# Pooled attention and a spatial gating unit on one core: gated units over other batches, and PSUM divided anew

## The chip, the cores and the metric

The kernel is one program on 1 core of one Trainium2 chip. A core has five engines with instruction queues of their own: TensorE (PE, matmuls, with weight loads shown apart as PEld), VectorE (DVE), ScalarE (ACT), GpSimd (POOL) and SyncE (SP, which here issues all DMA transfers). Each executes its own queue in order; semaphores tie the queues together. TensorE writes its products to PSUM, which the kernel divides into eight banks of 128 partitions x 512 float32; VectorE and ScalarE read them there. The metric is device microseconds for the whole program, as the median of several runs. One further execution is profiled; its instructions, with start and end, are the trace.

## The reference

What is computed is an attention with pooled queries, followed by a gated feed-forward block with a product over the sequence:

```python
q_pool = q.reshape(B, H, S // 2, 2, D).mean(axis=3)          # B=8, H=8, S=1152, D=64
scores = 1/sqrt(D) * q_pool @ k^T                            # 576 x 1152 for each batch and head
attn = exp(scores - max) / (sum + 1e-9)
x = (attn @ v), heads side by side                           # 8 x 576 x 512
h = maximum(x @ w_in, 0);  u, v = halves of h                # 512 columns each
v_n = (v - mean) / sqrt(var + 1e-6)                          # over the 512 columns
v_s = einsum('ts,bsd->btd', w_spatial, v_n) + b_spatial[None, :, None]   # over the 576 rows
out = (u * v_s) @ w_out                                      # 8 x 576 x 512
```

Inputs and outputs are float32, `w_in` and `w_out` come as 64-bit numbers whose two halves the kernel unpacks itself. To keep precision, a matrix that enters TensorE is split into a float16 head and a float16 rest, and most products are sums of three matmuls (head x head, head x rest, rest x head).

## The kernel before, in words

**Pairs.** The attention is done in 32 *pairs* of heads (8 batches, 4 pairs each). `attention(i)` (L487 on) makes the scores of pair i in 18 steps: for each, two matmuls of 512 columns (L506, L507) into a bank `pss`, an exponential on ScalarE (L512) and, for two steps together, a subtraction on GpSimd that makes the rest (L524). The remaining 64 query columns of each head go through four short `tail_tile`s (L520). `values` (L428, L432, L435) multiplies the exponentials with v into the bank `o`, four steps later; VectorE divides (`xm`, L443). `turn_main` (L457, L463) transposes a finished pair into `xg`, the input of the gated part (ScalarE L401, VectorE L402). `tail_values` (L478 to L480) does the short columns, in 27 matmuls.

**Beside each pair** small generators are advanced at fixed rates, once or more per *tick* (a pair has 40): `maxima` of the next pair (27 matmuls of 384 columns, L342 and L333, each reduced by VectorE at L348), `prep` of the pair after that (splitting q and k, with a scale that comes from a sum over partitions by TensorE, `scales`, L112), `values_ahead` (v), and until pair 8 `load_weights`, which fetches 512 x 512-column pieces of `w_in` and `w_out`, unpacks each with six VectorE and two ScalarE instructions (`from_double`, L149 to L161; the piece's staging is double-buffered) and splits it into head and rest (L135, L138). It is advanced by 0.25 steps a tick.

**Gated units.** A unit takes two batches, [0,1], [2,3], [4,5], [6,7]. `gated_unit` is a generator too: v products in nine row tiles (L582; ScalarE L590 evacuates, VectorE takes statistics at L592, L593), u products in 12 column pieces (L646, evacuated by ScalarE at L656) with the normalisation of v between (VectorE L618, L624, ScalarE L623), eight spatial products (L688 for 512 and L689 for 64 columns, into two banks at once; VectorE L695, L698), `split` (a scale of the gated product, `scale_of`, then head L135 and rest L138), output products in nine tiles (L731, evacuated by ScalarE at L751) and stores. A unit becomes ready when its last pair is transposed, and half a step of the oldest ready unit is made per tick; the unit's 160 or so steps so fill the eight pairs that follow. The last unit has no pairs beside it: it runs after pair 31, in two groups whose second scale lies behind the first group's products, and takes its banks from `pss` too.

**PSUM.** Eight banks: three `pss` (scores), two `pm` (maxima, scales, transposes, short columns), one `o`, two `pw` (units; while no unit is ready, every second maximum too).

**Order.** The code is written as one sequence, but a scheduler then sets the order on each engine: it keeps program order as priority and brings ready work forward, by its own estimate of durations and by which banks and buffers are free.

## Time and profile before

| | us |
|---|---|
| median of 3 runs | 1376.04 |
| lowest, highest | 1375.12, 1377.23 |
| the profiled execution | 1378.83 |
| its span, first to last instruction | 1377.1 |

| engine | busy us | share of the span | instructions |
|---|---|---|---|
| PE (matmuls) | 1222.1 | 89% | 13696 |
| PEld (weight loads) | 741.5 | 54% | 13696 |
| DVE | 967.1 | 70% | 2068 |
| ACT | 970.6 | 70% | 1632 |
| POOL | 847.0 | 62% | 492 |

Of the busy times it has to be known that matmuls are pipelined: a matmul's duration reaches from its start to its modelled end, and the next one starts long before that. So the distance from start to start, not the duration, is what a matmul takes of TensorE, and a busy TensorE is not one at its peak. The page's share is a mean over stages, so the stages are told apart with windows. In a row of a group, after the shapes and the count, stand the busy time and the mean of one in ns, then the time for which the engine had nothing to do before these instructions and what ended it. Waits are put down to what came last.

### The profile page before, as it was taken

The numbers are of one execution on the slowest core, as the hardware profiler recorded it, in microseconds if no ns is written. First come the engines' busy times: TensorE is split into PE (matmuls) and PEld (weight loads), VectorE is DVE, ScalarE is ACT, GpSimd is POOL, SyncE is SP. The second block draws the span as 40 slices with busy tenths as digits, with TensorE's granted clock in tenths as the row PEclk, the third lists the DMA queues.
The fourth block names the chain that finished last, engine by engine and source line by source line (L and its number), as shares of the span: only waits on it lengthen the run. The fifth ranks groups of instructions, "written<-read, shape, count | busy, mean of one in ns | idle before, by whom it ended". The sixth has DMA issues, their size and how long they took to land.

```text
span 1377.1 us, 33478 instructions
## 1 busy us (share of the span) xinstructions
PE 1222.1 (89%) x13696; PEld 741.5 (54%) x13696; DVE 967.1 (70%) x2068; ACT 970.6 (70%) x1632; POOL 847.0 (62%) x492
## 2 busy tenths in 40 slices
PE   3677887788998999889998999889998999899998
PEld 1354555555554665556555666555555566556443
DVE  5799889986869767765668766775667866761455
ACT  6777678779966777768776886768776776655333
POOL 3587677878755666657774766667666576655000
PEclk9998899989999999999999999999999999999999
DMA  7533343434333231244332132244331131101002
GB/s 252 166 97 109 94 124 94 128 93 139 113 96 96 79 94 56 62 126 135 96 96 87 51 91 84 74 118 135 104 96 42 47 94 55 28 24 40 8 1 69
DMA packets 56346, 123.77 MB, mean 90 GB/s; under 512 B 8256, under 2 KB 16448, under 8 KB 56192
## 3 DMA queue, kind: packets, MB, share of 16 engines
q1 hardware_dynamic: 56192, 121.63, 29.8%
q8 instruction: 107, 1.75, 0.5%
q14 instruction: 47, 0.39, 0.1%
HBM read 83.56 MB, written 9.44 MB: 68 GB/s over the span
## 4 chain that ended last, share of the span: by engine, by line
PE 47%; DVE 25%; ACT 8%; POOL 7%; DMA 7%; issue 4%; SPq 1%; POOLq 0%; ACTq 0%; DVEq 0%
DVE mt L348 7%; PE pss L507 5%; PE pss L506 5%; PE pw L688 5%; POOL pt L524 4%; PE pm L342 4%; PE pw L731 4%; PE pw L646 3%; PE o L435 3%; PE o L428 3%; PE pw L582 3%; ACT pt L512 3%; DMA kq<-in_qT_dram 3%; PE o L432 3%; DVE vv L138 2%
## 5 line engine op out<-in xcount | busy, mean ns | idle before, releaser
L524 POOL TENSOR_TENSOR pt<-pt 128x1024 f16<-128x1024 f32 x288 | 567.8, 1977 | 265.9 <-ACT pt L512 253.8
L512 ACT ACTIVATE pt<-pss,lnp,esc 128x512 f32<-128x512 f32 x576 | 439.4, 776 | 156.7 <-PE pss L507 148.1
L348 DVE TENSOR_REDUCE mt<-pm 128x1 f32<-128x384 f32 x730 | 395.8, 552 | 139.1 <-PE pm L342 119.2
L435 PE MATMUL o<-vp,pt 128*128 128x65 f16 x2304 | 282.8, 198 | 20.2 <-POOL pt L524 19.9
L428 PE MATMUL o<-vp,pt 128*128 128x65 f16 x2304 | 284.8, 196 | 13.0 <-DVE xm L443 12.8
L506 PE MATMUL pss<-qhi,khi 128*128 128x64 f16 (+1 forms) x1152 | 279.6, 294 | 9.1 <-ACT pt L512 8.0
L432 PE MATMUL o<-vp,pt 128*128 128x64 f16 x2304 | 284.5, 196 | 0.0
L507 PE MATMUL pss<-xq,klo 66*128 66x64 f16 (+1 forms) x1152 | 280.6, 295 | 4.1 <-DMA xq<-mr 4.1
L428 PEld LDWEIGHTS <-pt 128*128 128x128 bf16 x2304 | 222.7, 101 | 85.1 <-DVE xm L443 22.0
L432 PEld LDWEIGHTS <-pt 128*128 128x128 bf16 x2304 | 221.6, 100 | 50.7 <-issue 10.5
L342 PE MATMUL pm<-khi,qhi 128*128 128x384 f16 x652 | 217.9, 335 | 32.6 <-DVE mt L348 27.7
L435 PEld LDWEIGHTS <-pt 128*128 128x128 f16 x2304 | 220.7, 100 | 31.6 <-POOL pt L524 24.8
L507 PEld LDWEIGHTS <-klo 66*128 66x128 f16 x1152 | 99.1, 100 | 48.8 <-issue 17.3
L132 ACT ACTIVATE klo<-kq 128x1152 f16<-128x1152 f32 x64 | 74.6, 1166 | 63.7 <-DMA kq<-in_kT_dram 49.4
L506 PEld LDWEIGHTS <-khi 128*128 128x128 f16 x1152 | 103.5, 100 | 27.9 <-issue 12.2
L342 PEld LDWEIGHTS <-qhi 128*128 128x128 f16 x768 | 76.8, 101 | 66.3 <-issue 28.5
L524 POOL TENSOR_TENSOR ptl<-ptl 128x1152 f16<-128x1152 f32 x32 | 71.1, 2221 | 57.9 <-ACT ptl L520 57.9
L305 POOL TENSOR_TENSOR klo<-kq,khi 128x640 f16<-128x640 f32 x64 | 85.1, 1341 | 20.1 <-ACT khi L304 19.8
L520 ACT ACTIVATE ptl<-pss,lnp,esc 128x256 f32<-128x256 f32 (+1 forms) x128 | 75.6, 591 | 24.8 <-PE pss L507 24.2
L264 POOL TENSOR_TENSOR vp<-vt,vp 128x576 f16<-128x576 f32 x64 | 80.6, 1264 | 20.3 <-ACT vp L262 20.3
L582 PE MATMUL pw<-wi_h,xg 128*128 128x512 f16 x240 | 90.1, 382 | 0.0
L731 PE MATMUL pw<-wo_h,vv 128*128 128x512 f16 x216 | 80.3, 381 | 4.7 <-DVE vv L138 4.7
(177 smaller groups left out, 2394.2 us busy)
## 6 DMA issues: line engine op xcount, KB each, us to landing
vt<-in_v_dram SPq DMA_DIRECT2D x64, 576.0 KB
kq<-in_kT_dram SPq DMA_DIRECT2D x32, 576.0 KB
kq<-in_qT_dram SPq DMA_DIRECT2D x32, 576.0 KB
khi<-khi SPq DMA_DIRECT2D x96, 144.0 KB
out_dram<-row SPq DMA_DIRECT2D x24, 256.0 KB
qhi<-xq SPq DMA_DIRECT2D x64, 72.0 KB
klo<-klo SPq DMA_DIRECT2D x32, 144.0 KB
vv<-in_w_in_dram SPq DMA_DIRECT2D x8, 512.0 KB
```

Of the source, the lines that this page charges most:

```text
L305: nc.gpsimd.tensor_sub(KL[:, 0, a:z], k0[:, a:z], khh[:, 1, a:z])
L342: nc.tensor.matmul(pm[:, :W], lhsT=qhl[:, h, c0 : c0 + P], rhs=khh[:, h, n * NB : (n + 1) * NB, :], start=True, stop=True,)
L348: nc.vector.reduce_max(out=mt[:, t, n : n + 1], in_=pm[:, :W], axis=AX.X)
L428: nc.tensor.matmul(o[:, t], lhsT=top[:, cols], rhs=vp[:, D : D + D1], start=c == 0 and t == 0, stop=False, skip_group_check=True,)
L432: nc.tensor.matmul(o[:, t, 0:D], lhsT=top[:, cols], rhs=vp[:, 0:D], start=False, stop=False, skip_group_check=True)
L435: nc.tensor.matmul(o[:, t], lhsT=rst[:, cols], rhs=vp[:, D : D + D1], start=False, stop=c == NC - 1, skip_group_check=True,)
L506: nc.tensor.matmul(o, lhsT=khh[:, h, c, :], rhs=qhl[:, h, q], start=True, stop=False)
L507: nc.tensor.matmul(o, lhsT=KL[0:KR, h, c, :], rhs=X[0:KR, h, q], start=False, stop=True)
L512: nc.scalar.activation(pt, ps, AF.Exp, bias=lnp, scale=esc)
L524: nc.gpsimd.tensor_sub(t.bitcast(F16)[:, :, 0::2], t, t.bitcast(BF16)[:, :, 1::2])
L582: nc.tensor.matmul(ph, lhsT=xa[:, cc, c0 : c0 + P], rhs=wa[:, cc, DH:DF], start=n == 0, stop=n == 3 * NCC - 1,)
L731: nc.tensor.matmul(py, lhsT=ga[:, fc, c0 : c0 + P], rhs=wa[:, fc, :], start=m == 0, stop=m == end - 1)
```

## The change

The diff, cut to what matters:

```diff
--- before.py
+++ after.py
-    NU = B // 2
-    WS_STEPS = 2
-    MOE_RATE = 0.5
+    UNITS = [(0,)] + [(b, b + 1) for b in range(1, B - 1, 2)] + [(B - 1,)]
+    UNIT_OF = {b: (n, e) for n, bs in enumerate(UNITS) for e, b in enumerate(bs)}
+    NU = len(UNITS)
+    MOE_RATE = [0.36] + [0.5] * (NU - 1)
     D1 = D + 1
     VW = 2 * D + 2
+
+    W_RATE = 0.3
+    W_AT = 4
...
     ps_m = ctx.enter_context(tc.tile_pool(name="ps_m", bufs=2, space=PSUM))
+    ps_x = ctx.enter_context(tc.tile_pool(name="ps_x", bufs=1, space=PSUM))
     ps_o = ctx.enter_context(tc.tile_pool(name="ps_o", bufs=1, space=PSUM))
-    ps_w = ctx.enter_context(tc.tile_pool(name="ps_w", bufs=2, space=PSUM))
+    ps_w = ctx.enter_context(tc.tile_pool(name="ps_w", bufs=1, space=PSUM))
...
-        pt = ps_m.tile([P, 512], F32, name="pm")
+        pt = ps_x.tile([P, 512], F32, name="px")
...
-        lo, hi = src[:, 0::2], src[:, 1::2]
+        lo, hi = src.bitcast(U32)[:, 0::2], src[:, 1::2]
         V.tensor_scalar(out=t1, in0=hi, scalar1=0xFFFFF, scalar2=None, op0=ALU.bitwise_and)
         nc.scalar.activation(dst, t1, AF.Copy, bias=1.0, scale=2.0 ** -20)
-        V.tensor_scalar(out=t2, in0=lo, scalar1=1, scalar2=None, op0=ALU.logical_shift_right)
-        yield
-        V.scalar_tensor_tensor(out=dst, in0=t2, scalar=2.0 ** -51, in1=dst, op0=ALU.mult, op1=ALU.add)
+        yield
+        V.scalar_tensor_tensor(out=dst, in0=lo, scalar=2.0 ** -52, in1=dst, op0=ALU.mult, op1=ALU.add)
...
+    def load_matrix(name, w, wh, wl, a, x0):
+
+        st = vv0[:, V_FREE : V_FREE + 1024].bitcast(I32)
+        t1, t2 = (vv0[:, V_FREE + 1024 + j * 512 : V_FREE + 1536 + j * 512].bitcast(I32) for j in range(2))
+        n = w.shape[0] // P
+        sq = const.tile([P, n], F32, name=name + "q")
+
+        def fetch(c):
+            nc.sync.dma_start(out=st.bitcast(I64), in_=w[c * P : (c + 1) * P, a : a + 512])
+
+        fetch(0)
+        yield
+        for c in range(n):
+            d = u0[:, x0 + c * 512 : x0 + (c + 1) * 512]
+            yield from from_double(d, st, t1, t2)
+            if c + 1 < n:
+                fetch(c + 1)
+            square_sum(sq[:, c : c + 1], d, t1.bitcast(F32))
...
+        yield from load_matrix("wiv", w_in, wi_h, wi_l, DH, 0)
+        ready.add("wiv")
+        yield from load_matrix("wiu", w_in, wi_h, wi_l, 0, U_FREE)
+        ready.add("wiu")
+        yield from load_spatial()
+        ready.add("ws")
+        yield from load_matrix("wo", w_out, wo_h, wo_l, 0, U_FREE)
+        ready.add("wo")
+
+    weights = Pace(load_weights(), W_RATE, W_AT)
+
+    def need(name):
+        while name not in ready:
+            weights.gen = step(weights.gen)
...
-                if units or (t + n) % 2:
+                if units or (t + n) % 3:
...
-        return i % (2 * NHP) == 2 * NHP - 1
+        b, hp = divmod(i, NHP)
+        return hp == NHP - 1 and b == UNITS[UNIT_OF[b][0]][-1]
...
-        ps = ps_m.tile([P, 512], F32, name="pm")
+        ps = ps_x.tile([P, 512], F32, name="px")
...
+        bs = UNITS[un]
+        nb = len(bs)
+        cols = nb * S
+
+        tiles = [(j * P, [(bs[0], j * P, 0, P)]) for j in range(4)]
+        if nb == 2:
+            tiles.append((MAIN, [(bs[0], MAIN, 0, TAIL), (bs[1], MAIN, TAIL, P)]))
+            tiles += [(MAIN + P + j * P, [(bs[1], j * P, 0, P)]) for j in range(4)]
+            pieces = ((0, MAIN), (MAIN, MAIN + P), (MAIN + P, S2))
+        else:
+
+            tiles.append((S - P, [(bs[0], MAIN, TAIL, P)]))
+            pieces = ((0, S // 2), (S // 2, S))
...
-            if last and turn[0] % 5 > 1:
+            k = 5 if scores_left[0] else turn[0] % 6
+            if k < 3:
                 return ps_s.tile([P, MAIN], F32, name="pss")
+            if k < 5:
+                return ps_m.tile([P, 512], F32, name="pm")
             return ps_w.tile([P, 512], F32, name="pw")
...
+        need("wiv")
+        r_h = row_scales("wiv")
...
+        need("wiu")
+        r_h = row_scales("wiu")
+        u = u0[:, :U_FREE] if un == 0 else mo.tile([P, NT * DH], F32, name="u")[:, : NFC * cols]
...
-            pv = bank()
-            pvt = bank()
-            for n, (l, r) in enumerate(terms):
-                fl = dict(start=n == 0, stop=n == len(terms) - 1)
-                nc.tensor.matmul(pv, lhsT=l, rhs=r[:, 0:MAIN], **fl)
-                nc.tensor.matmul(pvt[:, :TAIL], lhsT=l, rhs=r[:, MAIN:S], **fl)
-                if n % 3 == 2:
-                    yield
-            m0, tl0 = (0, MAIN) if e == 0 else (MAIN + P, MAIN + TAIL)
             gg = wk.tile([P, DH], F32, name="row")
-            for a, n, pz, ba in ((m0, MAIN, pv, 0), (tl0, TAIL, pvt, MAIN)):
+            for a, z in ((0, S // 2), (S // 2, S)):
+                pv = bank()
+                for n, (l, r) in enumerate(terms):
+                    nc.tensor.matmul(
+                        pv[:, : z - a], lhsT=l, rhs=r[:, a:z], start=n == 0, stop=n == len(terms) - 1
+                    )
+                    if n == len(terms) // 2:
+                        yield
+                g = gg[:, : z - a]
                 nc.vector.scalar_tensor_tensor(
-                    out=gg[:, :n], in0=pz[:, :n], scalar=r_v, in1=b_bc[:, ba : ba + n], op0=ALU.mult, op1=ALU.add
+                    out=g, in0=pv[:, : z - a], scalar=r_v, in1=b_bc[:, a:z], op0=ALU.mult, op1=ALU.add
...
-                    t = mo.tile([P, NT, DH], F32, name="vv").rearrange("p a b -> p (a b)").bitcast(F16)
-                gt.extend(t.rearrange("p (l k t) -> p l k t", l=2, t=S2)[:, l] for l in range(2))
+                    t = vv.rearrange("p t d -> p (t d)")
...
-            credit = min(credit + MOE_RATE, 2.0)
+            weights.tick()
+            if units:
+                credit = min(credit + MOE_RATE[units[0][0]], 2.0)
             while credit >= 1 and units:
                 credit -= 1
                 unit_step()
...
+    scores_left[0] = False
     while todo or later:
         turn(last=True)
-    for g in units:
-        drain(g)
+    while units:
+        drain(units.pop(0)[1])
...
```

In words:

- **Units** now take [0], [1,2], [3,4], [5,6], [7]. The first is ready after pair 3. It is advanced by 0.36 steps a tick, the others by 0.5. Units of one batch have half the tiles; their u pieces have 288 + 288 columns. When the pairs are over, what is left of [5,6] and then [7] is drained; [7] has the two groups that [6,7] had. `gt` of a unit that isn't the last now is the tile `vv` itself.
- **Weights** come from one generator, advanced by 0.3 steps a tick over all pairs until it ends, in the order: v half of `w_in`, u half, spatial weights, `w_out`. Each half has a scale of its own (`wiv`, `wiu`). A unit that needs one which isn't there runs the generator up to it (`need`). A piece has one staging buffer, fetched anew when the piece is unpacked. One of the six VectorE instructions of a piece (L151) is gone: the low half is read as unsigned in the next.
- **PSUM**: three `pss`, two `pm` (maxima only), one `px` (scales, transposes, short columns), one `o`, one `pw` (units; every third maximum while no unit is ready). After the pairs a unit takes `pss`, `pm` and `pw` in turn.
- **The spatial product** is made in two halves of 288 columns, one after the other, each in one bank and read by VectorE before the next half begins in the same bank.

The rows below are the engines' orders, as the scheduler set them. First, VectorE in pair 0, before: work on the weights (L149 to L161, tiles `vv` and `u`), maxima (`mt`), and the scale of v (L127 to L122).

```order
L149 TENSOR_SCALAR vv<-vv 128x512
L161 TENSOR_TENSOR u<-u,vv 128x512
L348 TENSOR_REDUCE mt<-pw 128x1 x2
L151 TENSOR_SCALAR vv<-vv 128x512
L155 TENSOR_SCALAR vv<-vv 128x512
L348 TENSOR_REDUCE mt<-pw 128x1 x12
L153 SCALAR_TENSOR_TENSOR u<-vv,u 128x512
L127 TENSOR_REDUCE vt<-vsq 128x1
L117 TENSOR_SCALAR vh<-pm 128x1
L121 TENSOR_SCALAR vs<-vh 128x1
L122 TENSOR_SCALAR vr<-vh 128x1
L348 TENSOR_REDUCE mt<-pm 128x1 x13
```

And the same place in the changed kernel, from the end of the first piece on:

```order
L177 SCALAR_TENSOR_TENSOR u<-vv,u 128x512
L179 TENSOR_SCALAR vv<-vv 128x512
L183 SCALAR_TENSOR_TENSOR vv<-vv 128x512
L185 TENSOR_TENSOR u<-u,vv 128x512
L407 TENSOR_REDUCE mt<-pw 128x1
L407 TENSOR_REDUCE mt<-pm 128x1 x2
L407 TENSOR_REDUCE mt<-pw 128x1
L407 TENSOR_REDUCE mt<-pm 128x1 x3
```

Before, the second piece stands among the maxima, and those in `pm` come behind the scale of v; now the maxima of both kinds of bank follow the first piece at once, and the second piece comes behind them all. Counted over VectorE's order, five pieces have their first instruction within pair 0 before (up to the second L443), three now (up to the second L502); in pairs 1 to 3 it is three before and four now, with four of the head-and-rest steps beside them that came later before; in pairs 4 to 7 four before and five now, with 12 head-and-rest steps before and nine now, five of these for the spatial weights.

Second, TensorE at the border of two v tiles of a unit (L582 before, L663 now; `pw`). Before:

```order
L582 MATMUL pw<-wi_h,xg 128x512
L506 LDWEIGHTS khi_116
L506 MATMUL pss<-qhi_119,khi_116 128x512
L507 LDWEIGHTS klo_107
L507 MATMUL pss<-xq_113,klo_107 128x512
L342 LDWEIGHTS qhi_120
L342 MATMUL pm<-khi_117,qhi_120 128x384
L582 LDWEIGHTS xg
L582 MATMUL pw<-wi_h,xg 128x512
```

Now:

```order
L663 MATMUL pw<-wi_h,xg 128x512
L565 LDWEIGHTS khi_120
L565 MATMUL pss<-qhi_123,khi_120 128x512
L566 LDWEIGHTS klo_111
L566 MATMUL pss<-xq_117,klo_111 128x512
L415 MATMUL px<-ident,mx 9x128
L565 LDWEIGHTS khi_120
L565 MATMUL pss<-qhi_123,khi_120 128x512
L566 LDWEIGHTS klo_111
L566 MATMUL pss<-xq_117,klo_111 128x512
L663 LDWEIGHTS xg
L663 MATMUL pw<-wi_h,xg 128x512
```

Before, the first matmul of the new tile goes to the other of two banks, which was left a whole tile earlier; now it goes to the bank into which the matmul at the top wrote, four products and a short one earlier.

Third, TensorE after pair 31 at the scale of [5,6] (`gt`, L137), in the changed kernel: the end of the last spatial product (L771), the scale, the first output products (L821).

```order
L771 MATMUL pss<-ws_h,te 128x288
L771 LDWEIGHTS vv
L771 MATMUL pss<-ws_l,vv 128x288
L137 MATMUL px<-gt,ones 128x1
L821 LDWEIGHTS vv
L821 MATMUL pss<-wo_h,vv 128x512
L821 LDWEIGHTS vv
L821 MATMUL pss<-wo_l,vv 128x512
L821 LDWEIGHTS vv
L821 MATMUL pm<-wo_h,vv 128x512
```

Before, this scale of a unit that isn't the last stood between matmuls of the attention; nothing of [7] stands in this place, its v products (L663) follow the outputs of [5,6].

203 lines of the change are left out of this document (102 added, 101 removed).

## The prediction

> **What bounds the kernel now.** I read the page's utilisation first, then one table of windows by stage, then the waits of TensorE, and last the chain of waits at both ends. Two rows of the page, the busy tenths in 40 slices:
>
> ```profile
> PE   3677887788998999889998999889998999899998
> DVE  5799889986869767765668766775667866761455
> ```
>
> TensorE is far from full in the first nine slices, where VectorE is near full, and near full afterwards. The windows cut the span at the ends of head pairs (the second L443 of a pair): pair 0, pairs 1 to 3, 4 to 7, 8 to 10, pair 11, one full gated unit (16 to 23), the first two pairs of the last paced unit, the last two pairs, and what follows pair 31. Columns: length, then busy time of PE, PEld, DVE, ACT, POOL, granted clock, DMA share, GB/s.
>
> ```profile
> 0.00:88.90 88.90, 49.31 (x447) 26.54 (x447) 64.75 (x134) 62.76 (x115) 46.58 (x38) 1.00 0.62 196
> 88.90:192.90 104.00, 83.61 (x1048) 55.22 (x1046) 89.39 (x165) 76.45 (x129) 78.08 (x44) 0.87 0.38 109
> 192.90:333.70 140.80, 112.70 (x1426) 74.63 (x1426) 124.39 (x238) 112.32 (x190) 110.96 (x61) 0.89 0.36 104
> 333.70:462.10 128.40, 117.02 (x1272) 70.47 (x1270) 95.63 (x210) 98.80 (x173) 80.14 (x47) 0.95 0.31 92
> 462.10:500.00 37.90, 36.81 (x447) 22.94 (x446) 23.27 (x57) 31.54 (x53) 26.87 (x18) 1.00 0.29 87
> 654.80:971.30 316.50, 295.72 (x3424) 181.25 (x3423) 217.62 (x489) 233.56 (x390) 208.52 (x121) 0.98 0.31 91
> 971.30:1051.10 79.80, 73.19 (x834) 44.77 (x833) 51.99 (x129) 55.98 (x90) 53.48 (x32) 1.00 0.30 86
> 1213.50:1270.30 56.80, 55.34 (x698) 34.71 (x696) 18.09 (x45) 30.77 (x44) 32.61 (x18) 0.98 0.12 39
> 1270.30:1377.10 106.80, 102.84 (x609) 49.40 (x607) 52.78 (x121) 37.22 (x70) 0.00 (x0) 1.00 0.07 25
> ```
>
> So there are three regimes. In pairs 1 to 7 (35.0 us each) VectorE is busy 86% to 88%. With a gated unit beside the pairs (316.5 / 8 = 39.6 us each) TensorE is busy 93%. After pair 31 (106.8 us) TensorE alone counts: 102.84 us of matmuls for one unit of two batches, so a batch of gated work is about 51 us of TensorE and 26 us of VectorE.
>
> **The change, part by part.** Before, paced units have batches 0 to 5 and run in pairs 8 to 31; batches 6 and 7 come after. Now unit [0] runs in pairs 4 to 10, [1,2] in 12 to 19, [3,4] in 20 to 27, the first half of [5,6] in 28 to 31, and its second half and [7] come after: the same six batches and the same two. Only where the first six stand is different, and what each of them waits for. Cutting the spatial product in 288 + 288 instead of 512 + 64 columns costs nothing on TensorE, as starts show:
>
> ```profile
> 1329.65 0.38 PE L688 MATMUL pw<-ws_l,vv 128*128 128x512 f16 x1
> 1329.87 0.19 PE L689 MATMUL pss<-ws_l,vv 128*128 128x64 f16 x1
> 1329.89 0.38 PE L688 MATMUL pw<-ws_h,vv 128*128 128x512 f16 x1
> ```
>
> 0.22 us go to 512 columns and 0.02 to 0.03 to 64, so time goes by columns, and 576 stay 576.
>
> *Weights, pairs 0 to 7.* Per piece of 512 columns of doubles VectorE runs six instructions (in pairs 1 to 7):
>
> ```profile
> L161 DVE TENSOR_TENSOR u<-u,vv 128x512 f32<-128x512 f32 x8 | 13.3, 1660 | 0.1
> L159 DVE SCALAR_TENSOR_TENSOR vv<-vv 128x512 int32<-128x512 int32 x8 | 12.5, 1564 | 5.9 <-ACT vv L157 5.9
> L155 DVE TENSOR_SCALAR vv<-vv 128x512 int32<-128x512 int32 x7 | 10.4, 1482 | 0.0
> L151 DVE TENSOR_SCALAR vv<-vv 128x512 int32<-128x512 int32 x7 | 8.9, 1277 | 0.0
> L153 DVE SCALAR_TENSOR_TENSOR u<-vv,u 128x512 f32<-128x512 int32 x7 | 8.1, 1161 | 0.2
> L149 DVE TENSOR_SCALAR vv<-vv 128x512 int32<-128x512 int32 x7 | 6.2, 887 | 0.0
> ```
>
> Together 8.0 us; L151 goes, 6.75 stay. But the single staging buffer and the new pace move pieces later: in VectorE's order five first instructions of a piece (L149) stood within pair 0, now three (L174). Pair 0 is lightened, and weight work sits on its chain of waits:
>
> ```profile
> 45.46 0.53 ACT u L150
> 46.01 1.45 DVE u L153
> 50.25 2.00 DVE vv L151
> 52.25 0.48 DVE mt L348
> ```
>
> From 45.5 to 52.3 us the chain is weight pieces ahead of a maximum, 6.8 us; with the second piece later and shorter I take -8 for pair 0 (0 to -14). Pairs 1 to 3 get four pieces in place of three: 4 x 6.75 - 3 x 8.0 = +3, and four of the head-and-rest steps (about 1.2 us each), +8 in all on an engine with 14.6 us idle there: +5 (0 to +10). That the next fetch starts only after a piece is unpacked I cost at nothing: maxima stand between pieces in the order; a late one (a load's chain step takes 5 us) would hold VectorE, which the upper bound has.
>
> [...]
>
> *Unit [0], pairs 4 to 11.* Its VectorE work costs more beside GpSimd than alone; L618 in the paced part, and after pair 31:
>
> ```profile
> L618 DVE TENSOR_SCALAR row<-vv,mv,rs 128x512 f32<-128x512 f32 x27 | 28.1, 1049 | 0.3
> L618 DVE TENSOR_SCALAR row<-vv,mv,rs 128x512 f32<-128x512 f32 x9 | 4.5, 543 | 0.0
> ```
>
> So 26 us of a batch become some 32; 4/7 of it, 18 us, fall in pairs 4 to 7, while pieces and heads there stay within 2 us of before. VectorE then has 124.4 - 2 + 18 = 140 us in a stretch of 140.8; at its 0.9 the four pairs take 156: **+15** (+5 to +22). TensorE gets 4/7 of 51 = 29 us there, which it has. Pairs 8 to 10 lose the spatial weights' load and have 2.5/7 of 51 us = 18 in place of 39 us of unit matmuls. With 21 us less on TensorE and weights nearly done, they fall to about 34.5 each: 103.5, **-25** (-15 to -30). Pair 11 has no unit; ScalarE's 31.5 us bind: **-6.5** (0 to -8).
>
> *Pairs 12 to 31.* Before 1270.3 - 500.0 = 770.3. Now two full units, 2 x 316.5 = 633, then 79.8 for the first two pairs of [5,6], then the last two, which carry the u products and normalisation in place of output products: 56.8 + 2 of TensorE + 5 for VectorE. 777: **+6.5** (0 to +12).
>
> *After pair 31.* The same matmuls, but [5,6] now meets its scale with no attention left to cover it. Chain and pieces:
>
> ```profile
> 1273.37 2.59 PE pw L582 x12
> 1349.39 0.77 DVE row L695
> 1352.64 0.38 PE pm L112 x2
> L135 ACT ACTIVATE xg<-u,gs 128x576 f16<-128x576 f32 x8 | 5.8, 764 | 2.6 <-DVE gs L121 2.6
> L138 DVE SCALAR_TENSOR_TENSOR xg<-u,gs,xg 128x576 f16<-128x576 f32 x8 | 6.3, 817 | 2.2 <-ACT xg L135 2.2
> ```
>
> From a last spatial matmul to the end of the scale's is 3.6 us here, then a head and a rest, 1.6: some 5 us in which TensorE, whose order has nothing of [7] before the products, stands. The seven further pieces (5.7 us) are matched by two tiles' products (24 x 0.216 = 5.2). [7]'s own scales are covered as before. **+5** (0 to +10).
>
> *PSUM.* TensorE's waits in pairs 8 to 31, columns total, times, longest:
>
> ```profile
> PE pm L342 <- DVE mt L348: 20.1, 23, 2.2
> PE pm L333 <- DVE xg L402: 7.2, 3, 3.4
> PE pm L342 <- DVE xt L484: 3.1, 3, 1.1
> PE pw L689 <- ACT u L656: 2.8, 3, 1.1
> PE pm L333 <- DVE qkh L117: 2.4, 2, 1.2
> PE pw L689 <- DVE row L695: 1.2, 3, 0.5
> ```
>
> Maxima that wait for short work in their two banks (xg, xt, qkh: 12.7 us) cannot do so any more, and some of the 20.1 comes from one bank being taken: -12 to -36, I take -25. Against it, a unit's next group now starts in the bank that the last one just left. The order leaves four products and a short one between, some 1 us, where two banks left several. ScalarE evacuates 100 such groups (33 of v, 44 of u, 23 outputs); spatial halves are read by VectorE, whose wait was 1.2 us in all when both banks were taken at once, so nothing there. The evacuation:
>
> ```profile
> L590 ACT ACTIVATE vv<-pw,r_h x30: 667/687/713, 341.3 to 1289.0; 128x512 f32<-128x512 f32 x30
> ```
>
> 0.69 us and about 0.2 to start fit in 1 us unless ScalarE is busy, which it is 74% of the time; half an instruction of 0.69 x 0.74 is 0.25 us. **+25** (0 to 93, at L689's 2.8 / 3 = 0.93 each behind u). PSUM in sum: 0 (-36 to +80).
>
> The sum: -8 + 5 + 15 - 25 - 6.5 + 6.5 + 5 + 0 = **-8**: span 1377.1 to 1369. The profiled execution took 1378.83, 1.7 more than its span and 2.8 more than the median of the runs, 1376.04; so 1369 + 1.7 - 2.8 = **1368 us**.
>
> **Rivals.** *One bank for units binds.* For: the price behind u, 0.93. Against: L695's 1.2 us in 24 products. The mechanism decides from 0.33 us a group, where it eats the 8 us too; at 0.65, between there and 0.93, it is 40 more: 1408. [...] *Maxima go free.* All 36 us are won and unit groups wait for nothing: 1335. For: TensorE's largest wait there is L342's. Against: VectorE itself is late with maxima, and two banks stay two. *Early pairs give it all back.* Weight work and unit [0] meet on VectorE; pairs 4 to 7 lose 22 and pairs 8 to 11 win 22: 1368 + 7 + 9.5 = 1385. For: 88% busy. Against: the order has most weight steps done by pair 8.
>
> **Numbers.** The forecast 0.40, one bank 0.25, maxima free 0.20, given back 0.15. Its own range is 1353 to 1383. To leave out a fifth in all the range goes from 1338 to 1404. A measurement tells 0.2%, 2.75 us. Faster: 0.40 x 0.70 + 0.20 = 0.48; slower: 0.40 x 0.17 + 0.25 x 0.95 + 0.15 x 0.65 = 0.40; the rest, 0.12, within.
>
> **What would show it.** Windows of the changed kernel by the same pairs: 0 near 81, 4 to 7 near 156, 8 to 10 near 104, pair 11 near 31, the tail near 112. Waits of L342 and L392/L401 on xg, xt, qkh gone; waits of L663, L726, L821 on ScalarE's vv, u, row near 25 us in all. A wait of the first L821 of [5,6] near 5 us. I am wrong if pairs 12 to 27 take other than 316 +/- 8 a unit: then PSUM, not placement, made the time.

## The result and the profile after

The changed kernel takes 1437.45 us (median of 4 runs, 1433.91 to 1439.29) against 1375.58 us for the kernel before on the same chip: ratio 1.0446, 95% interval 1.0422 to 1.0470. That is 62 us slower, where 8 us faster was forecast, and outside the range of 1338 to 1404. The profiled execution has a span of 1434.7 us, 57.6 more than before.

Windows of the changed kernel, cut at the same places of the work as before (the end of the second multiply into xm of a pair, now L502). Columns as in the prediction: length, busy time of PE, PEld, DVE, ACT, POOL, granted clock, DMA share, GB/s. The rows are pair 0, 1 to 3, 4 to 7, 8 to 10, 11, then unit [1,2] beside pairs 12 to 19, unit [3,4] beside 20 to 27, pairs 28 to 31, and what follows.

```profile
0.00:77.60 77.60, 44.41 (x435) 25.01 (x435) 52.80 (x121) 57.58 (x105) 43.84 (x37) 0.87 0.65 203
77.60:186.60 109.00, 90.45 (x1081) 59.48 (x1079) 86.76 (x173) 84.61 (x144) 82.81 (x47) 0.84 0.37 110
186.60:349.20 162.60, 131.63 (x1591) 86.87 (x1591) 140.51 (x284) 128.70 (x223) 108.48 (x62) 0.96 0.37 109
349.20:462.20 113.00, 100.91 (x1225) 65.70 (x1223) 84.38 (x175) 84.88 (x142) 76.87 (x45) 0.97 0.34 99
462.20:490.60 28.40, 23.95 (x350) 16.17 (x348) 20.52 (x51) 24.27 (x39) 25.21 (x16) 1.00 0.33 95
490.60:825.20 334.60, 299.70 (x3418) 189.38 (x3419) 234.42 (x495) 238.50 (x396) 209.78 (x122) 0.97 0.29 87
825.20:1162.80 337.60, 304.84 (x3424) 192.52 (x3423) 233.68 (x496) 234.21 (x382) 209.24 (x121) 0.96 0.28 82
1162.80:1316.40 153.60, 139.59 (x1602) 86.18 (x1600) 88.34 (x198) 90.89 (x142) 87.80 (x49) 0.97 0.10 27
1316.40:1434.70 118.30, 110.38 (x664) 63.71 (x662) 53.02 (x128) 37.44 (x70) 0.00 (x0) 0.97 0.09 31
```

| stage | before, us | forecast | measured |
|---|---|---|---|
| pair 0 | 88.9 | -8 | -11.3 |
| pairs 1 to 3 | 104.0 | +5 | +5.0 |
| pairs 4 to 7 | 140.8 | +15 | +21.8 |
| pairs 8 to 10 | 128.4 | -25 | -15.4 |
| pair 11 | 37.9 | -6.5 | -9.5 |
| pairs 12 to 31 | 770.3 | +6.5 (and PSUM 0) | +55.5 |
| after pair 31 | 106.8 | +5 | +11.5 |

Up to pair 11 each term has the sign that was forecast, but together they give -9.4 us against -19.5. Most of the loss is in pairs 12 to 31. The kernel before has two such windows over the same pairs (12 to 19 and 20 to 27):

```profile
500.00:816.10 316.10, 294.24 (x3424) 180.77 (x3423) 217.93 (x488) 233.72 (x389) 208.41 (x121) 0.99 0.32 92
816.10:1130.80 314.70, 293.72 (x3424) 180.19 (x3423) 217.98 (x487) 230.56 (x381) 208.35 (x121) 0.99 0.30 88
```

The number of matmuls is the same, ScalarE and GpSimd are as busy as before, and VectorE does 16.5 us more in eight pairs with 7 to 9 instructions more (234.42 against 217.93), while the window is 18.5 us longer. So the first place to look is what VectorE's instructions take, not how many there are. TensorE's waits in pairs 12 to 31, changed kernel (the main rows; behind the colon us in all, times, longest us):

```profile
PE pm L401 <- DVE mt L407: 37.8, 32, 2.6
PE o L487 <- DVE xm L502: 14.2, 5, 5.5
PE pw L663 <- ACT vv L671: 7.3, 5, 1.9
PE px L522 <- DVE xg L461: 5.0, 3, 1.9
PE pw L726 <- ACT u L736: 4.6, 2, 2.5
PE pw L821 <- ACT row L841: 1.7, 4, 0.6
```

and the rows that answer to them in the kernel before, same pairs:

```profile
PE pm L342 <- DVE mt L348: 15.6, 18, 2.2
PE o L428 <- DVE xm L443: 5.3, 5, 1.4
PE pm L333 <- DVE xg L402: 3.7, 2, 1.9
PE pm L333 <- DVE qkh L117: 2.4, 2, 1.2
PE pm L342 <- DVE xt L484: 2.0, 2, 1.1
```

The waits of maxima on short work (xg, qkh, xt: 8.1 us here) are gone, as forecast; in their place short work waits for short work in its one bank (`px`, 5.0 us). The waits of unit groups on ScalarE are there: 7.3 + 4.6 + 1.7 = 13.6 us here, and some 16 us over the whole span, where 25 was forecast. But the wait of maxima on their own reductions went from 15.6 to 37.8 us, and that of the value products on xm from 5.3 to 14.2: VectorE is late.

Why it is late is seen in one place. VectorE just ahead of the longest of these waits, changed kernel, pair 14 (start, duration, instruction):

```profile
597.24 0.29 DVE L712 COPY te<-vv 64x512 f16<-64x512 f16 x1
597.54 1.89 DVE L711 COPY te<-vv 64x512 f16<-64x512 f16 x1
599.44 1.40 DVE L712 COPY te<-vv 64x512 f16<-64x512 f16 x1
600.87 2.27 DVE L705 TENSOR_TENSOR vv<-row,vv 128x512 f16<-128x512 f32 x1
...
604.10 0.41 DVE L502 TENSOR_TENSOR xm<-o,den 128x256 f32<-128x256 f32 x1
```

and TensorE behind it, with what it stood idle before the instruction in brackets:

```profile
604.57 0.24 PE L487 MATMUL o<-vp,pt 128*128 128x65 f16 x1 [5.46 <-DVE xm L502]
```

The first copy of te takes 0.29 us, the next two of the same size 1.89 and 1.40. GpSimd's instructions of this stretch end at 599.28 and 600.69 us, and these two copies end 0.15 us behind each of them. The same instruction has two prices. Durations in ns (least, median, most) of two lines of VectorE over the whole execution, changed kernel:

```profile
L346 DVE SCALAR_TENSOR_TENSOR esc<-qkr x32: 143/1184/2025, 9.0 to 1205.9; 128x1 f32<-128x1 f32 x32
L407 DVE TENSOR_REDUCE mt<-pm x806: 520/557/560, 19.1 to 1270.5; 128x1 f32<-128x384 f32 x162
```

L346 multiplies one number per partition, operands and result in SBUF: 143 ns at least, but 1184 at the median and 2025 at most. L407 reads PSUM, and none of its 806 instances exceeds 560. By start times, 17 of the 32 instances of L346 begin while a GpSimd instruction runs and average 1502 ns; the other 15 average 155. The GpSimd instruction is mostly this one, 1.96 us each:

```profile
L583 POOL TENSOR_TENSOR pt<-pt 128x1024 f16<-128x1024 f32 x288 | 563.4, 1960 | 337.1 <-ACT pt L571 318.7 <-DVE mx L411 10.8 <-DVE mt L407 3.0
```

That gave theory L: a VectorE instruction whose operands are all in SBUF stands until GpSimd's running instruction is over, one that reads PSUM does not, and the change moved VectorE's work so that more of it meets GpSimd, ahead of reductions that TensorE waits for. The first part is too wide as it stands: the reciprocals of `den` (L467, 128x4), in SBUF alone, take 179 ns at most, though 38 of 64 begin while GpSimd works, and neither reductions (L411, at most 184 ns) nor statistics (L673, 678 to 697 ns) in SBUF ever take long. It holds in the trace of the change for multiplies (L785, 128x288: 445 ns at least, 1720 at most), subtractions (L705: 656 and 2384), copies (L711: 275 and 1889) and work on exponents (`qks`, L146: 160 and 2068).

The traces bear out the last part. In pairs 12 to 31 of the kernel before, 57 VectorE instructions run over 0.3 us past the least of their line and shape, by 64.7 us in all; in the changed kernel it is 90, by 104.4 us. None of them reads PSUM, and all but one begin while a GpSimd instruction runs. The rival was the division of PSUM itself (theory P, its form with the single unit bank B).

### The profile page after: what moved, and what is told of

It is laid out like the page before. It is cut to its first block, busy times and chain, and to the rows that moved or that the text cites. A ratio compares the mean times of both kernels' runs of the same rounds, so it can differ in the third digit from the quotient of the medians.

```text
span 1434.7 us, 33721 instructions
## 1 busy us (share of the span) xinstructions
PE 1245.9 (87%) x13772; PEld 785.0 (55%) x13772; DVE 994.4 (69%) x2109; ACT 981.1 (68%) x1635; POOL 844.0 (59%) x492
## 4 chain that ended last, share of the span: by engine, by line
PE 52%; DVE 26%; ACT 9%; DMA 4%; issue 4%; POOL 3%; SPq 1%; POOLq 0%; ACTq 0%; DVEq 0%
DVE mt L407 8%; PE pss L565 6%; PE pss L566 6%; PE pm L401 5%; PE pw L771 5%; PE pw L663 4%; ACT pt L571 3%; PE pw L726 3%; PE pw L821 3%; PE o L487 3%; PE o L494 3%; PE o L491 3%; DVE qhi L163 2%; DMA kq<-in_kT_dram 2%; PE pss L771 2%
## 5 line engine op out<-in xcount | busy, mean ns | idle before, releaser
L407 DVE TENSOR_REDUCE mt<-pm 128x1 f32<-128x384 f32 x806 | 430.1, 552 | 150.0 <-PE pm L401 134.9
L401 PE MATMUL pm<-khi,qhi 128*128 128x384 f16 x716 | 240.5, 338 | 75.4 <-DVE mt L407 71.7
L487 PE MATMUL o<-vp,pt 128*128 128x65 f16 x2304 | 279.4, 196 | 18.3 <-DVE xm L502 18.3
L494 PE MATMUL o<-vp,pt 128*128 128x65 f16 x2304 | 278.5, 198 | 9.6 <-POOL pt L583 9.5
L491 PE MATMUL o<-vp,pt 128*128 128x64 f16 x2304 | 278.1, 195 | 0.0
L565 PEld LDWEIGHTS <-khi 128*128 128x128 f16 x1152 | 103.3, 101 | 57.2 <-issue 19.5
L663 PE MATMUL pw<-wi_h,xg 128*128 128x512 f16 x264 | 100.6, 383 | 8.2 <-ACT vv L671 8.1
L771 PEld LDWEIGHTS <-vv 128*128 128x128 f16 (+1 forms) x832 | 79.1, 99 | 41.0 <-issue 18.6
L364 POOL TENSOR_TENSOR klo<-kq,khi 128x640 f16<-128x640 f32 x64 | 86.9, 1366 | 24.7 <-ACT khi L363 24.6
L323 POOL TENSOR_TENSOR vp<-vt,vp 128x576 f16<-128x576 f32 x64 | 83.4, 1306 | 19.9 <-ACT vp L321 19.5
L726 PE MATMUL pw<-xg,wi_h 128*128 128x512 f16 (+2 forms) x360 | 87.6, 335 | 6.4 <-ACT u L736 5.2
```

Source lines behind the costliest of these rows:

```text
L401: nc.tensor.matmul(pm[:, :W], lhsT=qhl[:, h, c0 : c0 + P], rhs=khh[:, h, n * NB : (n + 1) * NB, :], start=True, stop=True,)
L407: nc.vector.reduce_max(out=mt[:, t, n : n + 1], in_=pm[:, :W], axis=AX.X)
L487: nc.tensor.matmul(o[:, t], lhsT=top[:, cols], rhs=vp[:, D : D + D1], start=c == 0 and t == 0, stop=False, skip_group_check=True,)
L491: nc.tensor.matmul(o[:, t, 0:D], lhsT=top[:, cols], rhs=vp[:, 0:D], start=False, stop=False, skip_group_check=True)
L494: nc.tensor.matmul(o[:, t], lhsT=rst[:, cols], rhs=vp[:, D : D + D1], start=False, stop=c == NC - 1, skip_group_check=True,)
L565: nc.tensor.matmul(o, lhsT=khh[:, h, c, :], rhs=qhl[:, h, q], start=True, stop=False)
```

## The experiments

All fourteen in one table; ratios are to the kernel before on the same chip. Edit S gives short VectorE work an operand in PSUM, edit T takes the copies of te to ScalarE; both are shown below.

| run | units and weights | product | PSUM | edits | median, us | ratio (95%) |
|---|---|---|---|---|---|---|
| (the change) | new | halves | new | | 1437.45 | 1.0446 (1.0422 to 1.0470) |
| e1 | new | halves | old | | 1412.38 | 1.0305 (1.0272 to 1.0337) |
| e2 | old | halves | old | | 1397.14 | 1.0185 (1.0161 to 1.0209) |
| e3 | old | halves | new | | 1463.81 | 1.0664 (1.0637 to 1.0692) |
| e4 | new | halves | new, 2 unit, 2 score banks | | 1426.15 | 1.0402 (1.0374 to 1.0430) |
| e5 | new | 512 + 64 | old | | 1400.93 | 1.0208 (1.0175 to 1.0241) |
| e6 | old | halves in PSUM | old | | 1369.94 | 0.9973 (0.9957 to 0.9990) |
| e7 | old | 512 + 64 | old | S | 1356.89 | 0.9893 (0.9864 to 0.9921) |
| e8 | new | halves | new | S | 1396.77 | 1.0154 (1.0100 to 1.0207) |
| e9 | new | halves | old | S | 1390.47 | 1.0128 (1.0088 to 1.0168) |
| e10 | new | halves | new, maxima and short work share 3 | | 1439.58 | 1.0482 (1.0435 to 1.0528) |
| e11 | old, L151 removed | 512 + 64 | old | S, T | 1343.83 | 0.9784 (0.9747 to 0.9821) |
| e12 | new | 512 + 64 | old | S | 1378.26 | 1.0032 (1.0011 to 1.0053) |
| e13 | new | 512 + 64 | old | S, T | 1366.34 | 0.9951 (0.9935 to 0.9967) |
| e14 | new | halves | new | S, T | 1389.20 | 1.0119 (1.0076 to 1.0161) |

**e1, the change with PSUM as before.**

```diff
-    ps_x = ctx.enter_context(tc.tile_pool(name="ps_x", bufs=1, space=PSUM))
-    ps_w = ctx.enter_context(tc.tile_pool(name="ps_w", bufs=1, space=PSUM))
+    ps_w = ctx.enter_context(tc.tile_pool(name="ps_w", bufs=2, space=PSUM))
...
-        pt = ps_x.tile([P, 512], F32, name="px")
+        pt = ps_m.tile([P, 512], F32, name="pm")
```

(The other users of `px` go back to `pm` likewise, and while no unit is ready every second maximum goes to `pw` again.)

> The changed kernel with PSUM divided as before: short work back on the two maxima's banks, two banks for units, every second score group of the stretch without units there. Units, weights' order and rates, and the spatial halves stay as changed. Theory P (the new division of PSUM made the loss in pairs 12 to 31): the time falls from 1437 to about 1390 (1376 + some 10), and a unit of eight pairs takes about 320 us again. Theory H (the new units, weights or halves made it, by VectorE's work falling behind GpSimd's more often): it stays above 1425, and eight pairs still take 330 or more. Between 1400 and 1420: both have a part.

1412: both have a part. PSUM makes 1.4% of the 4.5, units, weights and halves the other 3.05. Unit [1,2] takes 325.8 us beside its eight pairs, 9 less than with the new division and 10 more than before.

**e2, the kernel before with halves only.** Its spatial product is replaced by the loop over two halves of the diff; nothing else changes.

> The kernel before with the spatial product in two halves and nothing else changed. Theory H: the halves add about 4 us of VectorE's multiplying to each unit (15.5 against 11.5 us in the trace of the change) and take two banks one after the other; if that is on the path, 4 units make 1390 or more. Theory P: within 3 us of 1376.

1397: the halves alone cost 1.85%, 25 us, although TensorE's columns are the same (some 7 us of it are TensorE's own all the same, see the part on the prediction). VectorE's busy time rises from 967.1 to 1009.2 us on the page. The multiplies by u in the kernel before and in this one:

```profile
L698 DVE TENSOR_TENSOR u<-u,row x64: 215/682/1941, 495.5 to 1351.3; 128x512 f32<-128x512 f32 x32, 128x64 f32<-128x64 f32 x32
```

```profile
L702 DVE TENSOR_TENSOR u<-u,row x80: 210/990/2087, 485.6 to 1371.1; 128x288 f32<-128x288 f32 x48, 128x224 f32<-128x224 f32 x16, 128x64 f32<-128x64 f32 x16
```

The median rises from 682 to 990 ns although no piece is now longer than 288 columns.

**e3, the kernel before with the new PSUM and the halves it needs.** Diff of e1 the other way round, and halves.

> The kernel before with the new division of PSUM (and the halves that it needs, since a unit has one bank), units and weights as before. Theory P: about 1376 + 45 to 55 = 1420 to 1430, since all units of this kernel but a part of the last run in one bank. Theory H (units, weights): at most 1395, what the halves alone give.

1464, slower than either theory allowed, and slower than the change itself. The division costs 4.8% here (1.0664 less 1.0185) and 1.4% in the change. One price for "one bank" cannot be both; what it costs depends on what stands beside it. Counted as above, VectorE's long instructions in pairs 12 to 31 lose 134.4 us here, more than in any other run (106.7 in e2).

**e4, two banks for units, two for scores.**

```diff
-    ps_s = ctx.enter_context(tc.tile_pool(name="ps_s", bufs=3, space=PSUM))
+    ps_s = ctx.enter_context(tc.tile_pool(name="ps_s", bufs=2, space=PSUM))
...
-    ps_w = ctx.enter_context(tc.tile_pool(name="ps_w", bufs=1, space=PSUM))
+    ps_w = ctx.enter_context(tc.tile_pool(name="ps_w", bufs=2, space=PSUM))
```

> The changed kernel with two banks for units and two for scores instead of one and three; two for maxima alone and one for short work stay. Theory P1 (the loss of the division is the one bank of the units, whose groups wait about 25 us in all and delay what stands behind them): pairs 12 to 31 fall from 826 to about 780 to 800 and the time to 1390 to 1415, less what two score banks cost. Theory P2 (the loss is that maxima got two banks of their own and are now issued where their reductions can't follow, or VectorE's order): the time stays at 1430 or above, and the maxima's waits on their reductions stay near 70 us on the whole span.

1426, between the two. The waits on L663, L726 and L821 drop out of the long ones, the wait of maxima stays, and scores wait more for their banks (pairs 12 to 31, main rows):

```profile
PE pm L401 <- DVE mt L407: 36.9, 37, 1.9
PE o L487 <- DVE xm L502: 12.7, 3, 5.5
PE pss L565 <- ACT pt L571: 4.6, 11, 1.5
```

So the single unit bank is not what keeps the maxima waiting.

**e5, new units, weights' order and pace only.** e1 with the product in 512 + 64 columns.

> The changed kernel with PSUM divided as before and the spatial product in 512 + 64 columns as before: what is left of the change is the new units, the weights' order and pace, and the unpacking with one instruction less. If the parts add up (halves +25.7 on the kernel before, this kernel with halves 1412): about 1387. If the new units pay for themselves once the halves are gone: 1376 or less. If halves cost little here and placement is the loss: above 1400.

1401, 2.1%. The three parts of the change thus cost, by ratios and in this order: units and weights 2.1%, halves 1.0%, PSUM 1.4%. They do not simply add up: the halves cost 1.85% on the kernel before (e2). By stage, units and weights alone give pairs 0 to 11 in 486.1 us against 500.0, take 323.8 and 322.1 us for the two units of eight pairs (316.1 and 314.7 before) and 116.0 after pair 31 (106.8). The halves without PSUM lengthen pairs 12 to 31 from 792.8 to 799.9, and PSUM to 825.8. VectorE's long instructions lose 79.9 us there in e5, 88.1 in e1, 104.4 in the change.

**e6, halves with their first step left in PSUM.** This is e2 with one line changed: the result of times r_v plus b goes back to its bank, so the multiply reads it from PSUM and u from SBUF.

```diff
-                g = gg[:, : z - a]
+                g = pv[:, : z - a]
```

> The kernel before with halves, and the halves' first step (times r_v plus b) written back into its PSUM bank, so that the multiply by u reads one operand from PSUM. Same instructions, same count. Theory L (an instruction of VectorE whose operands are all in SBUF stands until GpSimd's running instruction is over; the halves have 20 such multiplies in a unit in place of 16, and their place meets GpSimd more often: 967 ns a multiply against 678): the multiplies fall to about 0.3 to 0.5 us, VectorE's busy time falls by some 45 us, and the time goes from 1397 to 1380 or less. Theory B (the halves cost by their two banks one after the other): the bank is held about 0.4 us longer, and the time stays at 1397 or rises.

1370: one operand's place takes 27 us off e2 and 45 us off VectorE's busy time (1009.2 to 964.5), both as theory L had them. With it the kernel is no slower than the one before; but that one's own product still reads both operands from SBUF, so this is not the price of the halves like for like (e9 has that). The same multiplies:

```profile
L702 DVE TENSOR_TENSOR u<-u,pw x67: 211/453/456, 486.9 to 1340.1; 128x288 f32<-128x288 f32 x41, 128x224 f32<-128x224 f32 x13, 128x64 f32<-128x64 f32 x13
```

The median falls from 990 to 453 ns and the longest from 2087 to 456. TensorE's waits for mt in pairs 12 to 31, e2 first and then e6:

```profile
PE pm L342 <- DVE mt L348: 30.9, 38, 2.2
```

```profile
PE pm L342 <- DVE mt L348: 19.7, 20, 2.2
```

The instructions that run over 0.3 us past their least fall from 94 to 57 in these pairs, and from 106.7 to 62.5 us; the reductions stand behind them in VectorE's order. Theory B, by which a bank held longer costs time, falls for this kernel.

**e7 and e8, edit S on the kernel before and on the change.** The exponent h stays in the PSUM bank that it is read from; the product of the two scales becomes a sum of exponents with one operand there (ESC is 2 to the -4, so the constants are exact); the multiply by u is as in e6. The counts of instructions stay.

```diff
-        h = sm.tile([P, n], I32, name=name + "h", bufs=2)
+        h = pt[:, 8 : 8 + n].bitcast(I32)
...
+        if name == "qk":
+            nc.vector.tensor_scalar(out=r[:, 1:2], in0=h[:, 1:2], scalar1=c, scalar2=-31 * c, op0=ALU.mult, op1=ALU.add)
+            nc.vector.scalar_tensor_tensor(
+                out=r[:, 0:1], in0=h[:, 0:1], scalar=c, in1=r[:, 1:2], op0=ALU.mult, op1=ALU.add
+            )
+            return s.bitcast(F32), r.bitcast(F32)
...
-        nc.vector.scalar_tensor_tensor(
-            out=esc, in0=r[:, 0:1], scalar=ESC, in1=r[:, 1:2], op0=ALU.mult, op1=ALU.mult
-        )
-        st["esc"] = esc
+        st["esc"] = r[:, 0:1]
...
-                    out=gg[:, :n], in0=pz[:, :n], scalar=r_v, in1=b_bc[:, ba : ba + n], op0=ALU.mult, op1=ALU.add
+                    out=pz[:, :n], in0=pz[:, :n], scalar=r_v, in1=b_bc[:, ba : ba + n], op0=ALU.mult, op1=ALU.add
```

> The kernel before with three kinds of short VectorE work given an operand in PSUM: the exponents and scales of queries and keys, the product of the two scales, and the multiply by the spatial product. Nothing is taken away. Theory L: these kinds stand behind GpSimd for some 40 us in the trace of before (12.7 + 12.2 + 14.8); what of it lies ahead of a maximum comes off: 1340 to 1362. Theory B: 1371 +/- 4, because VectorE is only 70% busy.

> The changed kernel with the same edit as the one before it. These kinds stand behind GpSimd for 23 + 23 + 19 = 65 us there. Theory L: 1437 falls to 1385 to 1410, more than the same edit takes from the kernel before, so that the distance between the two shrinks from 62 to 35 to 50. Theory B (one bank for units, which is held longer by the multiplies): 1430 or above, a distance of 65 or more.

1357 and 1397: the edit takes 1.1% from the kernel before and 2.9% from the change, and the distance between them shrinks from 62 to 40 us. The profiled execution of e8 was its fastest of four (1382.92 us against a median of 1396.77), so its trace understates it. Groups of lines in e8 (instances | busy us, mean ns), beside 28.4 and 27.9 us for qks and esc in the change:

```profile
L146 DVE TENSOR_SCALAR qks<-px 128x2 int32<-128x2 int32 x32 | 4.9, 153 | 0.6
L149 DVE SCALAR_TENSOR_TENSOR qkr<-px,qkr 128x1 int32<-128x1 int32 x32 | 4.7, 148 | 0.1
```

and two of its waits in pairs 12 to 31, against 37.8 and 14.2 in the change:

```profile
PE pm L403 <- DVE mt L409: 23.2, 25, 2.6
PE o L489 <- DVE xm L504: 6.8, 5, 1.8
```

**e9, edit S on the change with PSUM as before.**

> The changed kernel with PSUM divided as before (1412 by itself) and the edit that gives short VectorE work an operand in PSUM (which took 1437 to 1397 under the new division). It tells how the new division cost its 25 us. If by moving VectorE's work onto GpSimd's (blocked time went from 47.5 to 58 us a unit): most of it goes with the edit, and this takes 1388 to 1397. If by the one bank of the units itself (waits of v, u and outputs on ScalarE): the 25 us stay, and this takes 1368 to 1378.

1390. With edit S the new division of PSUM costs 1.0154 - 1.0128 = 0.3% with intervals that overlap, instead of 1.4%. Taken as they are, the ratios put some four fifths of its price down to VectorE standing behind GpSimd; the overlap makes that share rough. The halves are another matter. e12 below is this kernel with the product in 512 + 64 columns and takes 1.0032: with edit S the halves still cost 1.0%, as much as without it (e1 against e5). So in the kernel with new units their price cannot be put down to multiplies that stand behind GpSimd.

**e10, maxima and short work share three banks.** The pools ps_m and ps_x become one of three.

> The changed kernel with the two banks for maxima and the one for short work joined into three that both share; units keep one bank. If the strict division between maxima and short work costs: 1437 falls by 10 or more. If the one bank of the units costs: 1437 +/- 4. My prediction had the opposite sign for the first (maxima that wait for short work, 12.7 us, go back to waiting): then above 1445.

1440, 0.4% above the change with intervals that overlap: no clear difference. Whether maxima have banks of their own or share with short work has no effect that can be told here; the forecast's -25 for it, 1.8%, has no counterpart in any run.

**e11, the fastest.** The kernel before with edit S, edit T and the unpacking without L151 of the change's diff.

```diff
-                nc.vector.tensor_copy(out=te[0:TAIL, 0, :], in_=h[0:TAIL])
+                nc.scalar.activation(te[0:TAIL, 0, :], h[0:TAIL], AF.Copy)
```

> The kernel before with the edit that gives short VectorE work an operand in PSUM (1357 by itself), the unpacking of doubles with one instruction less, as in the change, and the four copies of te a unit on ScalarE. Theory L: the removed L151 frees 12 x 1.2 us of VectorE in pairs 0 to 7 where it is 87% busy, less what then waits at the next instruction: -5 to -12; the copies -1 to -2 a unit: 1338 to 1352. [...]

1343.83, 2.2% faster than the kernel before and, by the ratios, 6.3% faster than the change. Against e7 the trace gains 5.4 us in pairs 0 to 7 (315.0 against 320.4), where no unit runs yet, so it is the missing L151. In pairs 12 to 31 the copies on ScalarE gain nothing here (758.4 us against 756.8). The traces differ by 5 us and the medians by 13, since e7's profiled execution was its fastest.

**e12 and e13, new units alone with edit S, then S and T.**

> New units, weights' order and pace alone (PSUM and product as before; 1401 by itself) with the same edit. If the units' loss in pairs 12 to 31 (7.5 us a unit) is blocked VectorE work too: more than the 16 us that the edit took from the kernel before, 1370 to 1380. If it is the tail and the early pairs alone: 1382 to 1387.

> New units alone with the edit for short VectorE work (1378), and the four copies of te a unit on ScalarE. If the copies in VectorE's order cause the stall of 4.7 us a unit: 2.5 units in pairs 12 to 31 and one at the early pairs give -8 to -14, 1364 to 1370. If the stall only moves to the subtraction behind the copies: 1375 to 1379.

1378 and 1366, both where theory L put them. The copies of te, in VectorE's order, were the stall: TensorE's wait for xm in pairs 12 to 31 falls from 13.2 us in e12 (longest 4.5) to 5.9 (longest 1.8), and the two full units from 319.3 and 316.8 us to 311.4 and 310.8. The first of them, now below that of the kernel before (316.1 us):

```profile
481.50:792.90 311.40, 292.72 (x3413) 180.30 (x3413) 205.60 (x487) 239.18 (x402) 207.62 (x122) 0.99 0.32 94
```

With the same edits the old full units take 308.8 and 313.1 us (e11): both kinds now cost the same. What remains between e13 and e11 (22 us by the medians, 20 in the traces) is by stage: 8.9 after pair 31, 8.1 in pairs 12 to 31 (7.8 of it in pairs 28 to 31, beside the first half of [5,6]) and 3.0 in pairs 0 to 11 (where e11 has 478.5 and e13 481.5). The tail's share is the units' own: in every kernel with new units it is 115.4 to 119.2 us, with old ones 106.5 to 108.4.

**e14, the change with S and T.**

> The changed kernel, its PSUM and halves, with both edits (1397 with the first alone). If VectorE's standing behind GpSimd made its loss: below 1390. If units and one bank cost by themselves: 1392 or above.

1389.2 with runs from 1382.8 to 1392.8: the median lies 0.8 us below the first bound and the runs on both sides of it, so this does not decide. Against e13 the halves and the new PSUM still cost 1.7%. Here the single banks show, in pairs 12 to 31 (main rows):

```profile
PE pm L403 <- DVE mt L409: 18.3, 22, 2.6
PE pw L665 <- ACT vv L673: 7.1, 6, 2.0
PE px L518 <- DVE qkr L149: 6.9, 8, 3.0
PE pw L728 <- ACT u L738: 6.4, 4, 3.0
```

The wait for mt is back near that of the kernel before (18.3 against 15.6), while the unit bank (7.1 + 6.4) and the one bank for short work, which edit S holds longer (6.9), have some 20 us. These waits are not yet a price: with edit S alone the new PSUM costs 0.3% (e8 against e9) and the halves 1.0% (e9 against e12); with both edits they were not taken apart.

Like for like the change is still the slower kernel. Against e11, which has both edits and the shorter unpacking too, e14 is 45 us slower (3.4%), where the change was 62 us slower than the kernel before. So what edits S and T take away is about a quarter of the loss. VectorE's long instructions in pairs 12 to 31 still lose 20 us more in e14 than in e11 (62.9 against 42.8), which may hold a part of the rest; no run took those away.

## Why the prediction was wrong

**Where it failed.** By e5, e1 and the change, pairs 12 to 31 got 22.5 us from units and weights, 7.1 from the halves and 25.9 from PSUM; the forecast had +6.5, nothing and 0. The step that failed most is the -25 within PSUM's 0, for maxima that no longer wait for short work: they wait for VectorE, and VectorE got later. What the forecast left out in these pairs is the time that VectorE's instructions stand behind GpSimd's (64.7 us before, 104.4 in the change, counted as above).

**Pair 0 to 11: right in kind.** -8, +5, +15, -25, -6.5 came as -11.3, +5.0, +21.8, -15.4, -9.5. The fall in unit matmuls freed pairs 8 to 10 only in part: they run at 37.7 us a pair (113.0 / 3), not 34.5, with TensorE busy 89% and its clock at 0.97. The rival "early pairs give it all back" came nearer than the forecast: it had +22 and -22, and pairs 4 to 7 and 8 to 11 gave +21.8 and -24.9 (the forecast had +15 and -31.5).

**"Cutting the spatial product in 288 + 288 costs nothing on TensorE": not quite, and not the only engine.** The matmuls and their columns did not change, but time does not go by columns everywhere. The rows in the prediction are of matmuls over 128 partitions; each product has one term over 64. In the kernel before:

```profile
1330.36 0.19 PE L689 MATMUL pss<-ws_h,te 128*128 128x64 f16 x1
1330.48 0.39 PE L688 MATMUL pw<-ws_l,vv 64*128 64x512 f16 x1
1330.71 0.19 PE L689 MATMUL pss<-ws_l,vv 64*128 64x64 f16 x1
1330.83 0.39 PE L688 MATMUL pss<-ws_h,vv 128*128 128x512 f16 x1
```

On both sides of this term 64 columns take 0.12 us and not 0.03, and in the changed kernel the two matmuls of 288 columns at this place take 0.22 us each instead of 0.12, in either half. After pair 31 an undisturbed product takes 3.64 us from start to start before (1327.19 to 1330.83), and two halves take 3.85 in the change (1340.95 to 1344.80): 0.21 more, by which 32 products make some 7 us. And the step left out that the same cut makes 20 multiplies of 16 on VectorE, and in e2 those of 288 columns took 1066 ns in the mean, where in e6, with an operand in PSUM, none took over 456. On the kernel before the cut cost 25 us (e2), and 27 came back with the operand in PSUM (e6). With the new units it cost 1.0%, some 13 us, with edit S and without it; by this estimate 7 of these are TensorE's, the rest stays open. The prediction had L618's two prices on the table (1049 and 543 ns) and used them for unit [0] only.

**"Maxima that wait for short work cannot do so any more: -25": the step that failed.** Those waits did go, but maxima wait for VectorE, and VectorE did not get earlier; their wait on mt rose by 22 us in pairs 12 to 31 (15.6 to 37.8). Banks of their own did not shorten a wait whose end VectorE's order set. The prediction said so of the rival "Maxima go free" ("VectorE itself is late with maxima, and two banks stay two") and did not apply it to its own term. e10, where maxima and short work share their banks again, shows nothing of the term. (Its bound of 36 was also added up too high: 12.7 + 20.1 is 32.8.)

**"100 groups evacuated by ScalarE in one bank: +25": too large as a wait, and not the main loss.** The rows give 13.6 us in pairs 12 to 31 and some 16 over the whole span. The division's 1.4% shrank to 0.3% under edit S, so most of what it cost came with VectorE's work that met GpSimd's. The rival "one bank for units binds" had the sign, but its 1408 stops 29 us short, and two banks (e4) brought back 0.4% of the 4.5.

**"Two full units, 2 x 316.5": 39 us short.** They take 334.6 and 337.6 us. With neither PSUM nor product changed they take 323.8 and 322.1 (e5). The row at 597.5 us and e13 name the copies of te. I had written that a miss here would mean PSUM and not placement; of 41 us in the two units, placement and weights have 15, halves 8 and PSUM 18.

**After pair 31: +5 came as +11.5.** The wait on the scale of [5,6] is there, and then one on the first head, as TensorE's waits after pair 31 show:

```profile
PE px L137 <- DVE gt L152: 2.3, 1, 2.3
PE pss L821 <- ACT vv L160: 1.3, 1, 1.3
```

That is 3.6 of the 5 forecast. Units alone make 9.2 of the 11.5 (e5); what the rest of it is, and a cure, were not tried.

## What to carry to other kernels

Ask of each VectorE instruction where its operands are. Here, with GpSimd busy some 60% of the time, a 150 ns instruction with all operands in SBUF took up to 2 us (L346, 143 to 2025 ns), and everything behind it in the order waited too; one operand left in PSUM took that away (456 ns at most in e6, 148 and 153 in the mean in e8). Which instructions do so is to be read from the trace, since reciprocals and reductions did not. The halves left TensorE's columns as they are and still moved VectorE's multiplies against GpSimd's work (25 us in e2), so the price of such an edit is to be read per line from least and most, not from the mean. And in this kernel a freed bank paid nothing (e10, 0.4% with intervals that overlap), since the wait ended not with the bank but with an engine that was late.

## What the runs showed of the hardware

Not expected: that instructions of one or two numbers per partition stood behind GpSimd like long ones (L346, 143 to 2025 ns; L146 for `qks`, 160 to 2068), and that multiplies which read a result written back to PSUM were free of it (e6, none over 456 ns).

Half the clock was granted around many of TensorE's long waits. In the changed kernel, the wait at 599 us and the 3.3 us after it (the column before the DMA share is the granted clock; it is 1.00 just before the wait, and again from 608 us on):

```profile
599.10:604.60 5.50, 0.04 (x2) 0.03 (x2) 5.46 (x9) 2.67 (x5) 3.49 (x3) 0.69 0.01 1
604.60:607.90 3.30, 3.30 (x38) 2.84 (x39) 2.04 (x5) 0.76 (x3) 0.00 (x0) 0.50 0.01 1
```

In the 3.3 us after the wait 0.50 of the clock is granted. By the trace's record of the granted clock, pairs 12 to 31 have 11 such stretches of 3.4 or 6.8 us in the changed kernel (54.6 us in all) and 4 in the kernel before (17.1 us); each comes with a wait of 1.9 us or more (the shortest that stand alone are three of 1.9 us, at 831, 907 and 1168 in the changed kernel), or with several shorter ones, but not every such wait has one (those of 2.5 us at 641 and 2.2 us at 763 in the changed kernel have none). At half speed the 37.5 us more would be up to 19 us of matmuls lost, an upper bound since part of each stretch is the wait itself. With edit S 20.5 us of them are left (e8), where the waits are fewer too; no run changed the clock alone.
